# Two blocks of x laid in one run, four single blocks at the end of the first half of the GLU, and the second half's weights made among them

## The chip, the cores and the metric

The program runs on one core of one Trainium2 chip. Its time is the device time of the whole program in microseconds (us), from the first to the last instruction with what the device adds around them. Engines are written as in the profile: PE is TensorE (matrix products), with PEld its weight loads; DVE is VectorE, ACT is ScalarE, POOL is GpSimd, SP is SyncE, which only issues transfers. Each engine works through its own list of instructions in order, and waits where a semaphore tells it to.

## The reference, cut to what matters

```
x   = pooled_attention(q, k, v)              # 8 x 8 heads, 576 queries, 72 pooled keys -> x is 4608 x 512
h   = x @ w_in                               # 4608 x 2048
g   = (a0 + a1 h + a2 h^2 + a3 h^3) / (1 + |b0| |h| + |b1| h^2 + 1e-6)
x2  = g @ w_out                              # 4608 x 512
out = eight experts over x2                  # each token to one expert by a global ranking of the logits
```

The change lies in the second stage (h, g and x2, the "GLU" below), where it runs beside the end of the attention and up to the start of the routing.

## The kernel before, in words

**Blocks and halves.** The 4608 tokens are 18 blocks of 256 (NB, BLK). The 2048 columns of h are taken in two halves (`half` 0 and 1) of four pieces of 256 (`fp` 0 to 3). The first half is made while attention delivers x, and its partial result for a block goes to DRAM (`ya_d`); so does x itself (`store_x`, to `x_d`). The second half brings x and the partial result back (`load_b` on POOL's queue, `load_ya` on SP's), adds its own part and makes the router's logits.

**A step.** One step is one piece `fp` of one block ("single", both 128-column groups of the piece for 256 tokens) or one 128-column group of a piece for two blocks ("pair", 512 tokens). Both fill one accumulator tile of 128 x 512. A step has four parts: `mm_h` (PE: x times w_in, each factor split in a high and a low part, three products per 128 rows of x, names xh, xl, wih, wil); `act1` and `act2` (the rational function: five operations on ACT, five on DVE, two on POOL, which end in a high and a low tile of g, "hi" and "lo", written by DVE at L729 and by POOL at L345); and `mm_y` (PE: hi and lo times w_out, woh and wol, one group per 128 tokens, "tt": a single has two of them, a pair four). In `mm_y` L793 and L794 read hi, L791 reads lo.

**The ring of hi/lo tiles.** `act2` writes into the next tile of the list `mgl`: five tiles `mg`, and five more, `mgx`, from block 4 on; in the second half `mgx` is closed and five tiles `gd` are opened once block 2 begins (`swap_g`). A tile comes free when the last `mm_y` group that reads it is done.

**Single blocks and pairs.** In the first half blocks 0 to 3 run single and 4 to 17 as pairs; in the second half 0 and 1 single (SINGLE = 2), the rest as pairs. The four x tiles are `xt[0]` (xh0, xl0) and `xt[1]` (xh1, xl1), each of two blocks; block by block they lie behind one another, so a pair's `mm_h` reads two runs of 256 columns (`x()[:, :, c, :]`).

**The weights.** They come as 64-bit numbers in pieces (`load_w`), and `prep_w` turns a piece into a high and a low part: on ACT a conversion, on DVE three passes (L410, L412, L414), ACT again (the high part), POOL (the low part), and for w_out also transposes and small products on PE (L432, L436), which give the columns for the router. Each half has four pieces `fp` with four `prep_w` calls each (k = 0, 1 for w_in, 2, 3 for w_out). Of the second half's sixteen, eight are made in the first half's last blocks, into the pool `wpb`, which is opened when attention's pool `ap` has been closed (block 15 of the first half must be done with its `mm_h` first); fp = 2 and 3 go into the tiles of the first half's fp = 0 and 1 and wait for its last `mm_y`.

**What sets the order.** Operations are recorded with a cost, and a planner (`Order.run`) puts each engine's into one list by these costs, the priorities and the tiles' dependencies. So the code gives what depends on what, and the printed order of each engine what stands where.

Of the kernel before, what the change touches and what calls it, by code (L numbers as in the profile page):

```python
# [30 lines left out]
BLK = 256  # L31
# [15 lines left out]
V_POOL = 0  # L47
GBUFS, MGX, GDX = 5, 5, 5
PTB = 2
# [30 lines left out]
class Part:  # L80
# [5 lines left out]
    def __call__(self):  # L86
        return self.buf()[:, self.j]


# [201 lines left out]
class Kern:  # L291
# [163 lines left out]
    def init_att(self):  # L455
# [423 lines left out]
    def load_b(self, n):  # L879

        s, j = n // 2 % 2, n % 2
        extra = [("xr", m) for m in range(NB) if m % XBUFS == j] if n < 2 else []
        for k, x in enumerate(self.x1[s]):
            self.op("Pool", 1.05, lambda k=k, x=x: self.nc.gpsimd.dma_start(x()[:, j], self.x_d[n]()[:, k]), r=[("xd", n, k)],
                    w=[("xs", s, j, k)] + extra, nbytes=524288)

    def phase1(self):
        nc, op, b = self.nc, self.op, self.buf
        nc.scalar.preload_act_table_set("natural_log_exp_and_others")
        for p in ("wq", "stg", "pre"):  # L890
            self.open(p, side="right")
        for p in ("wp", "mp", "xp", "xq", "ap"):
            self.open(p)
# [22 lines left out]

        pieces = {h: [(h, fp, k) for fp in range(NFP) for k in range(4)] for h in range(2)}
        loads = {h: list(pieces[h]) for h in range(2)}

# [30 lines left out]
        for i, st in enumerate(steps):  # L950
            st["i"] = i
            n = st["blk"]
            if st["half"] == 0:
# [4 lines left out]
                if n == SPLIT and st["first"] and st["half"] == 0:  # L958
                    self.swap_m()
                while done < needed[st["blks"][-1]]:  # L960
                    assert slot()
                if done < len(att):
                    credit += 4 * RATE
                    while credit >= 1.0 and done < len(att):
                        credit -= 1.0
                        if not slot():
                            credit = 0.0
                            break
                elif not closed and NB - 3 in xdone:
                    closed = True  # L970
                    reads = [k for k in self.g.lastw if self.in_pool(k, ("ap", "xq"))]
                    reads += [("xr", m) for m in range(NB) if m % XBUFS > 1] + [("x", m, s, k) for m in self.xkeys for s in range(2) for k in self.xkeys[m]]
                    def swap():
                        self.close("ap")
                        self.close("xq")
                        self.open("wpb")
                        self.open("raw1")
                    assert not pieces[0]
                    op("Z", 0.0, swap, w=reads + ["swap"])
                    for fp in range(2):  # L980
                        self.w_tiles(1, fp, "wpb", f"b{fp}")
                        for t in self.w[1, fp]:
                            for k in range(4):
                                self.g.lastw[t, k] = self.g.lastw["swap"]
                    self.staging("raw1")
                    for t in (*self.raws, *self.wf, self.wm):
                        self.g.lastw[t] = self.g.lastw["swap"]
                    for _ in range(2):
                        self.load_w(*loads[1].pop(0))
                if closed and pieces[1] and pieces[1][0][1] < 2:  # L990
                    piece(1)
                st["x"] = self.xb[n % XBUFS] if len(st["blks"]) == 1 else self.xt[n // 2 % 2]
                st["xk"] = [k for m in st["blks"] for k in self.xk(m)]
            else:
                if st["first"] and n == 0:
# [16 lines left out]
                x = self.x1[n // 2 % 2]  # L1012
                st["x"] = x if len(st["blks"]) == 2 else tuple(Part(t, n % 2) for t in x)
                st["xk"] = [("xs", n // 2 % 2, m % 2, k) for m in st["blks"] for k in range(2)]
# [73 lines left out]
    def swap_m(self):  # L1088
# [5 lines left out]
        self.more_g("mx", "swapm", MGX, "mgx")  # L1094

    def free_x(self, s):

        key = ("freex", s)
        self.op("Z", 0.0, lambda: None, w=[("xs", s, j, k) for j in range(2) for k in range(2)] + [key])
        new = [tuple(View(x, lambda t, j=j, i=i: t[:, j].rearrange("p (i c) t -> p i (c t)", i=2)[:, i]) for i in range(2))  # L1100
               for x in self.x1[s] for j in range(2)]
# [4 lines left out]
    def swap_b(self):  # L1106

        def swap():
            self.close("mx")
# [4 lines left out]
        self.op("Z", 0.0, swap, w=[k for k in self.g.lastw if self.in_pool(k, ("wq", "stg", "mx"))] + ["swapb"])  # L1114
        self.mgl = [g for g in self.mgl if g[0].pool != "mx"]
        x = tuple(self.buf("yp", [128, 2, 4, BLK], F32R, x) for x in ("xhr", "xlr"))
        self.x1 = [self.xt[0], x]
        for j in range(2):
            for k in range(2):
                self.g.lastw["xs", 1, j, k] = self.g.lastw["swapb"]  # L1120
        self.yab = self.ring(2, "yp", [128, 2, 2 * GW], F32, "yab")
# [15 lines left out]
    def swap_g(self):  # L1137
# [4 lines left out]
        self.op("Z", 0.0, swap, w=[k for k in self.g.lastw if self.in_pool(k, ("raw1",))] + ["swapg"])  # L1142
        self.more_g("gd", "swapg", GDX, "gd")
        more = self.ring(MORE_R, "gd", [128, 2 * BLK], F32, "mrg")
        self.mr += more
# [592 lines left out]
TWO = 2  # L1738
PAIRS = SPLIT
Y0 = 4  # L1740
# [85 lines left out]
```

## Time and profile before

| | |
|---|---|
| time, median of 3 runs (lowest, highest) | 1531.73 us (1530.30, 1533.25) |
| profiled execution: time, span | 1529.58 us, 1527.8 us |
| mean granted TensorE clock | 0.982 |
| PE busy | 1454.1 us, 95% of the span |
| DVE busy | 1097.6 us, 72% |
| ACT, POOL busy | 883.3 us, 58%; 865.0 us, 57% |

A busy share is the part of the span in which the engine had at least one instruction under way. The granted clock is a share of TensorE's full speed; its two levels are 1.2 and 2.4 GHz, so that a mean between 0.5 and 1 says for how much of a stretch the lower one held.

### The profile page before, as it was taken

What the parts mean: (1) busy time and instruction counts of PE and PEld (TensorE: products, weight loads), DVE (VectorE), ACT (ScalarE), POOL (GpSimd) and SP (SyncE); (2) the same over time, 40 slices, a digit from 0 to 9 for tenths busy, and PEclk for the clock granted to TensorE, in tenths of its full rate; (3) what the DMA queues carried; (4) which work ended last, traced back from release to release, by engine and by line L of the source; (5) the groups of instructions that cost most, each with busy time, mean ns of one, the idle gap of its engine ahead of it and who ended that gap; (6) DMA issues with size and microseconds to landing.
All of it is one profiled execution on the core that took longest, in us unless ns stands there. A gap on an engine that the chain in (4) does not pass through costs nothing. (4 is left out here: it accounts for less than half of the span.)

```text
span 1527.8 us, 27162 instructions
## 1 busy us (share of the span) xinstructions
PE 1454.1 (95%) x9353; PEld 1307.1 (86%) x9353; DVE 1097.6 (72%) x3105; ACT 883.3 (58%) x2071; POOL 865.0 (57%) x806
## 2 busy tenths in 40 slices
PE   8899999999999999989999999995999999999996
PEld 6899978888898998978898998764888988988995
DVE  6897786858768678688777778888788778941220
ACT  5887886867868766656655456841343432443330
POOL 6776877557657456545544455652465554654421
PEclk9999999999999999989999999998999999999998
DMA  6663534132321324523231332003254333433300
GB/s 223 220 226 105 170 123 148 58 130 94 132 102 49 112 73 163 168 82 107 85 103 65 111 108 87 29 29 123 75 172 143 133 114 125 156 114 112 128 18 31
DMA packets 82023, 173.62 MB, mean 114 GB/s; under 512 B 10320, under 2 KB 37328, under 8 KB 81872
## 3 DMA queue, kind: packets, MB, share of 16 engines
q1 hardware_dynamic: 70800, 134.02, 25.9%
q0 software_dynamic: 11072, 37.76, 7.5%
q8 instruction: 74, 1.21, 0.3%
q14 instruction: 77, 0.63, 0.1%
HBM read 122.28 MB, written 49.46 MB: 112 GB/s over the span
## 5 line engine op out<-in xcount | busy, mean ns | idle before, releaser
L345 POOL TENSOR_TENSOR mq<-mq,ms 128x512 f32<-128x512 f32 x144 | 195.1, 1356 | 151.1 <-ACT mq L711 149.2
L693 PE MATMUL pa<-xh,wih 128*128 128x512 f32 (+1 forms) x448 | 166.7, 372 | 4.2 <-ACT wih L351 1.7
L693 PE MATMUL pa<-xh,wil 128*128 128x512 f32 (+1 forms) x448 | 159.3, 356 | 0.8 <-POOL wil L345 0.8
L693 PE MATMUL pa<-xl,wih 128*128 128x512 f32 (+1 forms) x448 | 158.9, 355 | 0.0
L708 ACT ACTIVATE ms<-pa 128x512 f32<-128x512 f32 x144 | 85.8, 596 | 120.1 <-PE pa L693 88.8
L1664 PE MATMUL pa<-yth,w1h 128*128 128x320 f32 (+1 forms) x512 | 145.2, 299 | 1.1 <-ACT yth L1635 0.7
L1664 PE MATMUL pa<-ytl,w1h 128*128 128x320 f32 (+1 forms) x512 | 144.3, 297 | 0.0
L1664 PE MATMUL pa<-yth,w1l 128*128 128x320 f32 (+1 forms) x512 | 143.9, 296 | 0.0
L713 DVE TENSOR_TENSOR mw<-mw,pa 128x512 f32<-128x512 f32 x144 | 97.9, 680 | 54.9 <-ACT mw L709 54.0
L793 PE MATMUL pa<-woh,mg 128*128 128x260 f32 (+1 forms) x484 | 131.1, 293 | 5.0 <-DVE mg L729 2.7
L794 PE MATMUL pa<-wol,mg 128*128 128x260 f32 (+1 forms) x484 | 129.0, 289 | 0.0
L1717 POOL DMA_INDIRECT out<-ob,ix x40 | 38.9, 972 | 152.5 <-ACT ob L1713 130.1
L345 POOL TENSOR_TENSOR mg<-mt,mr 128x512 fp32r<-128x512 f32 x68 | 89.0, 1310 | 63.8 <-DVE mt L733 36.1
L711 ACT ACTIVATE mq<-ms,scal 128x512 f32<-128x512 f32 x144 | 117.8, 818 | 10.0 <-DVE mt L731 9.9
L726 ACT ACTIVATE mr<-mq,scal 128x512 f32<-128x512 f32 x122 | 88.5, 725 | 50.4 <-POOL mq L345 39.5
L709 ACT ACTIVATE mw<-pa,scal 128x512 f32<-128x512 f32 x144 | 112.3, 780 | 1.6 <-PE pa L693 1.2
L1667 ACT ACTIVATE h2h<-pa 128x256 fp32r<-128x256 f32 (+1 forms) x128 | 51.4, 410 | 103.8 <-PE pa L1664 96.9
L565 ACT ACTIVATE ex<-pa,nm 128x72 f32<-128x72 f32 (+2 forms) x320 | 98.5, 325 | 20.0 <-DVE nm L556 13.8
L714 DVE SCALAR_TENSOR_TENSOR pa<-mw,scal,pa 128x512 f32<-128x512 f32 x144 | 107.7, 748 | 3.0 <-ACT ms L708 1.5
L733 DVE SCALAR_TENSOR_TENSOR mt<-pa,scal,mt 128x512 f32<-128x512 f32 x144 | 106.8, 742 | 0.9
L1698 PE MATMUL pa<-w2h,h2h 128*128 128x512 f32 x256 | 102.2, 399 | 0.0
L1290 DVE TENSOR_SCALAR_CACHE_REDUCE BJ<-BQ,cand 128x288 uint16<-128x288 f32 x217 | 99.5, 509 | 3.4 <-ACT BQ L1470 1.5
(325 smaller groups left out, 4865.1 us busy)
## 6 DMA issues: line engine op xcount, KB each, us to landing
wraw<-in_w SPq DMA_DIRECT2D x64, 512.0 KB, 3.6
ya_d<-ya SPq DMA_DIRECT2D x18, 520.0 KB, 3.3
yab<-ya_d SPq DMA_DIRECT2D x18, 520.0 KB, 4.3
kvraw<-in_kT SPq DMA_DIRECT2D x16, 576.0 KB, 4.2
x_d<-xh SPq DMA_DIRECT2D x18, 512.0 KB, 3.4
x_d<-xl SPq DMA_DIRECT2D x18, 512.0 KB, 4.6
y_d<-yb SPq DMA_DIRECT2D x18, 512.0 KB, 3.0
raw<-in_w_in SPq DMA_DIRECT2D x16, 512.0 KB, 4.8
```

The costliest lines, as they stand in the source:

```text
L345: self.g.either({"Pool": (p_tt(n), lambda: nc.gpsimd.tensor_tensor(out(), x(), y(), op=alu)), "DVE": (c_tt(n), lambda: nc.vector.tensor_te ...
L565: op("Act", c_act(NK, 0, 1, 1), lambda h=h: nc.scalar.activation(e()[:n, h, :], sv()[:, h, :], AF.Exp, bias=nm()[:n, h:h + 1], accum_out=s ...
L693: nc.tensor.matmul(o, w()[:, c, f], x()[:, :, c, :] if two else x()[:, c, :], start=c == 0 and k == 0, stop=c == 3 and k == 2)
L709: op("Act", c_act(N, 0, 2), lambda: nc.scalar.activation(w(), ph(), AF.Identity, scale=self.a3(), bias=self.a2()), r=hk + self.sk, w=[w])
L711: op("Act", c_act(N, 1, 2), lambda: nc.scalar.activation(q(), s(), AF.Identity, scale=self.b1a(), bias=self.b0a()), r=[s] + self.sk, w=[q])
L714: op("DVE", c_stt(N), lambda: nc.vector.scalar_tensor_tensor(ph(), w(), self.a1(), ph(), op0=ALU.add, op1=ALU.mult), r=[w], w=hk)
L733: op("DVE", c_stt(N), lambda: nc.vector.scalar_tensor_tensor(t(), w(), self.a0(), t(), op0=ALU.add, op1=ALU.subtract), r=[(w, 0), self.hri ...
L793: nc.tensor.matmul(o, hi()[:, f], w(woh), start=first, stop=False)
L794: nc.tensor.matmul(o, hi()[:, f], w(wol), start=False, stop=False)
L1290: D(.43, lambda: self.nc.vector.tensor_scalar(j(), key(), cand(), None, op0=ALU.is_ge, op1=ALU.add, accum_out=self.cnt()[:, col:col + 1]), ...
L1664: nc.tensor.matmul(ps()[:, 0:n], w()[:, c, fs], x()[:, c, :], start=i == 0, stop=i == 11)
L1698: nc.tensor.matmul(ps(), x()[:, t], w()[:, f % 2, :], start=f == 0 and i == 0, stop=False)
```

## The change

Five things change together. (1) An x tile now holds the two blocks side by side for each 128 rows (`[128, 4, 2, BLK]` for `[128, 2, 4, BLK]`), so a pair's `mm_h` reads one run of 512 columns; writing a block, storing it and loading it touch four runs of 256 for one of 1024. (2) Blocks 14 to 17 of the first half run single (PEND = NB - 4), and the five `mgx` tiles are given back at block 14 (`swap_x`), so the ring has five tiles from there until block 2 of the second half. (3) `ap` is closed at block 14, once attention has been recorded to its end, and the second half's weights start there: ten pieces go into blocks 14 to 17 by one a step, some more in block 17's last steps, and the rest is recorded at the start of the second half. fp = 2 takes the tiles of w_in's fp = 0 and two new tiles in `wpb`, fp = 3 those of w_in's fp = 1 and of w_out's fp = 0; for fp = 2 w_out's pieces come first. (4) The second half's x goes to `xt[1]` first and then `xt[0]`, instead of `xt[0]` and two tiles xhr, xlr of its own. (5) Three tiles `gd` instead of five, and w_out's tiles of the first half's fp = 1 serve as two more.

```diff
-GBUFS, MGX, GDX = 5, 5, 5
+GBUFS, MGX, GDX = 5, 5, 3
...
+class Col(Part):
+
+
+    def __call__(self):
+        return self.buf()[:, :, self.j]
...
-        self.xt = [tuple(b(p, [128, 2, 4, BLK], F32R, f"{x}{k}") for x in ("xh", "xl")) for k, p in enumerate(("xp", "xq"))]
-        self.xb = [tuple(Part(x, k % 2) for x in self.xt[k // 2]) for k in range(XBUFS)]
+        self.xt = [tuple(b(p, [128, 4, 2, BLK], F32R, f"{x}{k}") for x in ("xh", "xl")) for k, p in enumerate(("xp", "xp"))]
+        self.xb = [tuple(Col(x, k % 2) for x in self.xt[k // 2]) for k in range(XBUFS)]
...
-            o = ph().rearrange("p (b t) -> p b t", b=2) if two else ph()[:, BLK * j:BLK * j + BLK]
+            o = ph() if two else ph()[:, BLK * j:BLK * j + BLK]
...
-                    nc.tensor.matmul(o, w()[:, c, f], x()[:, :, c, :] if two else x()[:, c, :],
+                    nc.tensor.matmul(o, w()[:, c, f], x()[:, c].rearrange("p b t -> p (b t)") if two else x()[:, c, :],
...
-        parts = alone + [(0, [n], range(NFP)) for n in range(SPLIT, PAIRS)] + [(0, [n, n + 1], range(NFP)) for n in range(PAIRS, NB, 2)]
+        parts = alone + [(0, [n], range(NFP)) for n in range(SPLIT, PAIRS)] + [(0, [n, n + 1], range(NFP)) for n in range(PAIRS, PEND, 2)]
+        parts += [(0, [n], range(NFP)) for n in range(PEND, NB)]
...
+                if n == PEND and st["first"]:
+                    while rest:
+                        rest.pop(0)()
+                    self.swap_x()
...
-                elif not closed and NB - 3 in xdone:
+                elif not closed and n >= PEND:
...
+                    free = [self.buf("wpb", [128, 2, 2, GW], F32R, f"{x}b2") for x in ("woh", "wol")]
+                    self.w[1, 2] = [*self.w[0, 0][:2], *free]
+                    self.w[1, 3] = [*self.w[0, 1][:2], *self.w[0, 0][2:]]
...
-                if closed and pieces[1] and pieces[1][0][1] < 2:
+                if closed and (len(pieces[1]) > 6 or len(pieces[1]) > 4 and n == NB - 1 and st["fp"] > 0 or len(pieces[1]) > 2 and n == NB - 1 and st["fp"] > 1):
                     piece(1)
...
-                    for fp in (2, 3):
-                        self.w[1, fp] = self.w[0, fp - 2]
-                while pieces[1] and pieces[1][0][1] <= st["fp"]:
-                    piece(1)
+                    while pieces[1]:
+                        piece(1)
...
+    def swap_x(self):
+        self.op("Z", 0.0, lambda: self.close("mx"), w=[k for k in self.g.lastw if self.in_pool(k, ("mx",))] + ["swapx"])
+        self.mgl = [g for g in self.mgl if g[0].pool != "mx"]
...
-        x = tuple(self.buf("yp", [128, 2, 4, BLK], F32R, x) for x in ("xhr", "xlr"))
-        self.x1 = [self.xt[0], x]
...
+        self.x1 = self.xt[::-1]
...
+        w = self.w[0, 1][2:]
+        self.op("Z", 0.0, lambda: None, w=[(t, k) for t in w for k in range(4)] + ["freew"])
+        new = [tuple(View(t, lambda t, i=i: t.rearrange("p c g d -> p (c g d)")[:, 512 * i:512 * i + 512]) for i in range(2)) for t in w]
...
-PAIRS = SPLIT
+PAIRS, PEND = SPLIT, NB - 4
```

ACT, DVE, POOL and SP have as many operations as before. PE's matmuls go from 9343 to 9535. Each engine's order is the same up to the first `mm_h` of block 14 in the first half (about 503 us in the trace) and again from block 2's last piece of the second half (about 715 us); between them it is another one. In the rows below lines of after.py stand seven higher (L693 is L700, L791 to L794 are L798 to L801, L345 is L352, L884 is L891).

On PE, where block 14 begins in the first half, the list before has a pair's `mm_h` (xh1, xl1 hold blocks 14 and 15) among the last `mm_y` groups of the pair 12 and 13.

```order
L552 MATMUL pa7_274<-kbd0_100,qraw0_102 128x144 x2
L693 MATMUL pa5_233<-xh1_795,wih0_145 128x512
L693 MATMUL pa5_233<-xl1_809,wih0_145 128x512
L693 MATMUL pa5_233<-xh1_795,wil0_191 128x512
L791 MATMUL pa4_231<-woh3_1595,mg4_1460 128x260
```

With the change the same place has the first products of block 14 alone, half as wide and twice as many.

```order
L559 MATMUL pa7_271<-kbd0_97,qraw0_99 128x144 x2
L700 MATMUL pa5_230<-xh1_792,wih0_142 128x256
L700 MATMUL pa5_230<-xl1_806,wih0_142 128x256
L700 MATMUL pa5_230<-xh1_792,wil0_188 128x256
L700 MATMUL pa5_230<-xh1_792,wih0_142 128x256
L700 MATMUL pa5_230<-xl1_806,wih0_142 128x256
L700 MATMUL pa5_230<-xh1_792,wil0_188 128x256
L798 MATMUL pa4_228<-woh3_1592,mg4_1457 128x260
```

The weights' names now say which piece they are: a pair's row carries 512 tokens against the weights loaded for it, a single's row 256. Over the whole program 192 rows of 128x512 have become 384 of 128x256.

On PE, where the second half begins (wihb0 is its first weight, woh3 the first half's last), the list before has the first `mm_h` of block 0 right behind products that read the last piece's hi and lo of the pair 16 and 17.

```order
L791 MATMUL pa5_233<-woh3_1595,mgx4_2868 128x260
L791 MATMUL pa3_197<-woh3_1595,mgx4_2868 128x260
L793 MATMUL pa5_233<-woh3_1595,mg1_981 128x260
L794 MATMUL pa5_233<-wol3_1607,mg1_981 128x260
L793 MATMUL pa3_197<-woh3_1595,mg1_981 128x260
L794 MATMUL pa3_197<-wol3_1607,mg1_981 128x260
L693 MATMUL pa4_231<-xh0_353,wihb0_6152 128x256
```

With the change that `mm_h` stands directly behind the last `mm_h` of the first half, and the `mm_y` groups of block 17 from its piece 1 on follow it.

```order
L700 MATMUL pa4_228<-xh0_350,wil3_1490 128x256
L439 MATMUL pa1_145<-ident_112,wf1_6171 128x128 x4
L700 MATMUL pa2_191<-xh1_792,wihb0_6150 128x256
L700 MATMUL pa2_191<-xl1_806,wihb0_6150 128x256
L700 MATMUL pa2_191<-xh1_792,wilb0_6166 128x256
L700 MATMUL pa2_191<-xh1_792,wihb0_6150 128x256
L700 MATMUL pa2_191<-xl1_806,wihb0_6150 128x256
L700 MATMUL pa2_191<-xh1_792,wilb0_6166 128x256
L800 MATMUL pa3_194<-woh1_625,mg4_1457 128x260
```

The first step of the second half now stands ahead of the `mm_y` of block 17's pieces 1 to 3 instead of among the pair's last ones, and its x comes from xh1 and xl1.

On POOL, where x of the second half's first two blocks is loaded (x_d0, x_d1), the list before has the loads among the low parts of the weights and of `mgx` tiles, late in the pair 16 and 17.

```order
L884 DMA xh0_353<-x_d0_594 128x1024
L345 TENSOR_TENSOR wolb1_6607<-wf0_6139,wohb1_6594 128x2x256
L345 TENSOR_TENSOR mgx3_2796<-mt0_889,mr1_934 128x512
L884 DMA xh0_353<-x_d1_813 128x1024
L884 DMA xl0_362<-x_d0_594 128x1024
L345 TENSOR_TENSOR mgx4_2868<-mt1_992,mr0_835 128x512
L884 DMA xl0_362<-x_d1_813 128x1024
```

With the change they go to xh1 and xl1, in pieces of four runs, among the low parts of block 14's and 15's steps, whose tiles are now the five `mg` alone.

```order
L891 DMA xh1_792<-x_d0_591 128x4x256
L352 TENSOR_TENSOR mg2_1158<-mt0_886,mr1_931 128x512
L352 TENSOR_TENSOR mq2_1002<-mq2_1002,ms1_872 128x512
L891 DMA xl1_806<-x_d0_591 128x4x256
L352 TENSOR_TENSOR mg3_1343<-mt1_989,mr0_832 128x512
L352 TENSOR_TENSOR mq0_763<-mq0_763,ms0_735 128x512
L352 TENSOR_TENSOR mg4_1457<-mt2_1192,mr1_931 128x512
L352 TENSOR_TENSOR mq1_891<-mq1_891,ms1_872 128x512
L352 TENSOR_TENSOR wilb0_6166<-wf0_6130,wihb0_6150 128x512
```

The first load stands some thirty rows earlier in POOL's list (row 409 for 442), ahead of the first low part of a second-half weight instead of behind the sixth.

## Rows read from the trace of the kernel before

**Rows 1.** The page: engines' busy time and share; granted clock in 40 slices, tenths.

```profile
PE 1454.1 (95%) x9353; PEld 1307.1 (86%) x9353; DVE 1097.6 (72%) x3105; ACT 883.3 (58%) x2071; POOL 865.0 (57%) x806
...
PEclk9999999999999999989999999998999999999998
```

**Rows 2.** Stretches, us: busy time (instructions) of each engine, granted clock, DMA.

```profile
core 0: us, PE busy (x) PEld busy (x) DVE busy (x) ACT busy (x) POOL busy (x), PEclk, DMA share, GB/s
...
505.00:692.00 187.00, 175.38 (x1188) 161.90 (x1187) 142.11 (x259) 118.82 (x223) 100.60 (x88) 0.96 0.37 124
...
580.00:596.00 16.00, 12.25 (x83) 11.22 (x82) 16.00 (x26) 12.64 (x23) 14.27 (x13) 0.95 0.42 138
596.00:604.00 8.00, 7.99 (x59) 7.50 (x59) 5.44 (x11) 3.68 (x10) 4.33 (x5) 0.88 0.76 252
604.00:620.00 16.00, 16.00 (x136) 16.00 (x136) 6.33 (x12) 7.38 (x15) 6.37 (x7) 1.00 0.59 199
...
636.00:662.00 26.00, 19.87 (x110) 17.29 (x109) 18.06 (x29) 18.29 (x34) 14.84 (x14) 0.82 0.38 122
662.00:692.00 30.00, 28.27 (x196) 26.06 (x196) 26.43 (x67) 10.41 (x16) 11.14 (x8) 0.99 0.21 71
...
960.00:1000.00 40.00, 40.00 (x177) 30.81 (x176) 39.42 (x81) 37.17 (x60) 27.88 (x20) 1.00 0.08 26
```

**Rows 3.** Waits of PE from 560 to 690 us: total, times, longest.

```profile
PE pa L432 <- DVE wf L414: 2.6, 1, 2.6
PE pa L693 <- ACT wih L351: 1.7, 1, 1.7
```

**Rows 4.** Timeline of PE at the half switch: start, duration, group, idle before.

```profile
588.69 0.39 PE L793 MATMUL pa<-woh,mgx 128*128 128x260 f32 x1 [0.85 <-DVE mgx L729]
...
594.32 0.71 PE L791 MATMUL pa<-woh,mgx 128*128 128x260 f32 x2 [1.59 <-POOL mgx L345]
...
599.72 0.28 PE L693 MATMUL pa<-xh,wihb 128*128 128x256 f32 x1
...
600.31 0.28 PE L693 MATMUL pa<-xh,wilb 128*128 128x256 f32 x1
```

**Rows 5.** Timeline of PE in a pair's products of 512.

```profile
568.49 0.39 PE L693 MATMUL pa<-xh,wil 128*128 128x512 f32 x1
...
572.22 0.40 PE L693 MATMUL pa<-xh,wih 128*128 128x512 f32 x1
```

**Rows 6.** Timeline of PE in the experts' products of 512, from one run.

```profile
1400.30 0.39 PE L1698 MATMUL pa<-w2h,h2h 128*128 128x512 f32 x1
...
1403.29 0.39 PE L1698 MATMUL pa<-w2h,h2l 128*128 128x512 f32 x1
1403.51 1.98 PE L1695 MATMUL pa<-w2l,h2h 128*128 128x512 f32 x8
```

**Rows 7.** Groups of PE over the span, shapes apart: count, busy, mean ns.

```profile
L693 PE MATMUL pa<-xh,wih 128*128 128x512 f32 x288 | 118.1, 410 | 1.9 <-ACT ex L565 1.2 <-DVE pth L594 0.5
...
L693 PE MATMUL pa<-xhr,wihb 128*128 128x512 f32 x64 | 25.8, 403 | 0.2 <-DVE mt L733 0.2
```

**Rows 8.** Groups of the weight loads over the span.

```profile
L693 PEld LDWEIGHTS pa<-xh,wih 128*128 128x128 f32 x448 | 85.4, 191 | 15.5 <-ACT ex L565 2.0 <-ACT wih L351 1.9 <-ACT mr L728 0.9
```

**Rows 9.** Groups of DVE and POOL, 540 to 720 us, shapes apart.

```profile
L714 DVE SCALAR_TENSOR_TENSOR pa<-mw,scal,pa 128x512 f32<-128x512 f32 x26 | 19.4, 747 | 0.2
L713 DVE TENSOR_TENSOR mw<-mw,pa 128x512 f32<-128x512 f32 x26 | 17.6, 678 | 21.1 <-ACT mw L709 21.1
L410 DVE TENSOR_SCALAR pa<-wm 128x512 int32<-128x512 int32 x16 | 11.0, 689 | 5.0 <-ACT wm L409 4.8
...
L345 POOL TENSOR_TENSOR mgx<-mt,mr 128x512 fp32r<-128x512 f32 x5 | 6.5, 1291 | 3.5 <-DVE mt L733 3.0 <-ACT mr L728 0.5
```

**Rows 10.** Transfers of x: count, ns to issue min/median/max, first and last start.

```profile
L355 SPq DMA_DIRECT2D x_d<-xh x18: 320/359/559, 42.6 to 524.4; - x18
...
L884 POOL DMA_DIRECT2D xh<-x_d x10: 537/580/757, 591.0 to 932.8; - x10
...
DMA to landing us min/median/max: 2.6/4.5/8.8
```

More of the change, by code (lines that the diff above doesn't have):

```diff
@@ L881, in load_b @@
         s, j = n // 2 % 2, n % 2
-        extra = [("xr", m) for m in range(NB) if m % XBUFS == j] if n < 2 else []
+        extra = [("xr", m) for m in range(NB) if m % XBUFS == 2 - 2 * s + j] if n < 4 else []
         for k, x in enumerate(self.x1[s]):
-            self.op("Pool", 1.05, lambda k=k, x=x: self.nc.gpsimd.dma_start(x()[:, j], self.x_d[n]()[:, k]), r=[("xd", n, k)],
+            self.op("Pool", 1.05, lambda k=k, x=x: self.nc.gpsimd.dma_start(x()[:, :, j], self.x_d[n]()[:, k]), r=[("xd", n, k)],
                     w=[("xs", s, j, k)] + extra, nbytes=524288)
@@ L891, in phase1 @@
             self.open(p, side="right")
-        for p in ("wp", "mp", "xp", "xq", "ap"):
+        for p in ("wp", "mp", "xp", "ap"):
             self.open(p)
@@ L917, in phase1 @@
         pieces = {h: [(h, fp, k) for fp in range(NFP) for k in range(4)] for h in range(2)}
+        pieces[1][8:12] = [(1, 2, k) for k in (2, 3, 0, 1)]
         loads = {h: list(pieces[h]) for h in range(2)}
@@ L968, in phase1 @@
                             break
-                elif not closed and NB - 3 in xdone:
+                elif not closed and n >= PEND:
                     closed = True
-                    reads = [k for k in self.g.lastw if self.in_pool(k, ("ap", "xq"))]
-                    reads += [("xr", m) for m in range(NB) if m % XBUFS > 1] + [("x", m, s, k) for m in self.xkeys for s in range(2) for k in self.xkeys[m]]
+                    reads = [k for k in self.g.lastw if self.in_pool(k, ("ap",))]
+                    reads += ["swapx"]
                     def swap():
                         self.close("ap")
-                        self.close("xq")
                         self.open("wpb")
@@ L984, in phase1 @@
                                 self.g.lastw[t, k] = self.g.lastw["swap"]
+                    free = [self.buf("wpb", [128, 2, 2, GW], F32R, f"{x}b2") for x in ("woh", "wol")]
+                    self.w[1, 2] = [*self.w[0, 0][:2], *free]
+                    self.w[1, 3] = [*self.w[0, 1][:2], *self.w[0, 0][2:]]
+                    for t in free:
+                        for k in range(4):
+                            self.g.lastw[t, k] = self.g.lastw["swap"]
                     self.staging("raw1")
@@ L1012, in phase1 @@
                 x = self.x1[n // 2 % 2]
-                st["x"] = x if len(st["blks"]) == 2 else tuple(Part(t, n % 2) for t in x)
+                st["x"] = x if len(st["blks"]) == 2 else tuple(Col(t, n % 2) for t in x)
                 st["xk"] = [("xs", n // 2 % 2, m % 2, k) for m in st["blks"] for k in range(2)]
@@ L1099, in free_x @@
         self.op("Z", 0.0, lambda: None, w=[("xs", s, j, k) for j in range(2) for k in range(2)] + [key])
-        new = [tuple(View(x, lambda t, j=j, i=i: t[:, j].rearrange("p (i c) t -> p i (c t)", i=2)[:, i]) for i in range(2))
+        new = [tuple(View(x, lambda t, j=j, i=i: t[:, 2 * j + i].rearrange("p b t -> p (b t)")) for i in range(2))
                for x in self.x1[s] for j in range(2)]
@@ L1108, in swap @@
         def swap():
-            self.close("mx")
             self.close("stg")
@@ L1113, in swap @@
             self.open("yp", side="right")
-        self.op("Z", 0.0, swap, w=[k for k in self.g.lastw if self.in_pool(k, ("wq", "stg", "mx"))] + ["swapb"])
-        self.mgl = [g for g in self.mgl if g[0].pool != "mx"]
-        x = tuple(self.buf("yp", [128, 2, 4, BLK], F32R, x) for x in ("xhr", "xlr"))
-        self.x1 = [self.xt[0], x]
-        for j in range(2):
-            for k in range(2):
-                self.g.lastw["xs", 1, j, k] = self.g.lastw["swapb"]
+        self.op("Z", 0.0, swap, w=[k for k in self.g.lastw if self.in_pool(k, ("wq", "stg"))] + ["swapb"])
+        self.x1 = self.xt[::-1]
         self.yab = self.ring(2, "yp", [128, 2, 2 * GW], F32, "yab")
@@ L1143, in swap_g @@
         self.more_g("gd", "swapg", GDX, "gd")
+        w = self.w[0, 1][2:]
+        self.op("Z", 0.0, lambda: None, w=[(t, k) for t in w for k in range(4)] + ["freew"])
+        new = [tuple(View(t, lambda t, i=i: t.rearrange("p c g d -> p (c g d)")[:, 512 * i:512 * i + 512]) for i in range(2)) for t in w]
+        for t in (x for g in new for x in g):
+            self.g.lastw[t] = self.g.lastw["freew"]
+        self.mgl = new + self.mgl
         more = self.ring(MORE_R, "gd", [128, 2 * BLK], F32, "mrg")
```

## The prediction

> **What bounds the kernel now.** I read the page first: PE is busy for 95% of the span and the other engines for 57 to 72%, and the granted clock is full in all but three of the 40 slices [rows 1]. So the time is PE's list of products at its pitch, plus the few places where PE stands still or runs at the lower clock. Then I cut the trace into stretches. The reader is to see that the change's own stretch, 505 to 692 us, is one of those places: PE works 175.38 of its 187 us, so 11.62 are idle, nearly all of them in 580–596 (3.75), 636–662 (6.13) and 662–692 (1.73) [rows 2]. In the same stretches the granted clock is 0.95, 0.88, 0.82 and 0.99 (580–596, 596–604, 636–662, 662–692), which is time at 1.2 GHz after PE had been waiting; as work lost while busy that is 12.25 × 0.05 + 7.99 × 0.12 + 19.87 × 0.18 + 28.27 × 0.01 = 5.5 us. Together some 17.1 us are lost at the passage from the first half to the second.
>
> What PE waits for there is told by the chain of waits and the timeline: passes of DVE over a weight piece (2.6 us in one), the high part of a weight on ACT (1.7), DVE's hi (0.85) and POOL's lo (1.59) of a step [rows 3, 4]. So it is short of ready operands, not of work: DVE is busy 16.00 of 16 us in 580–596, and then 6.33 of 16 in 604–620 [rows 2]. It has its weight pieces and its steps in two heaps with a hole between, the hole being the last `mm_y` of the pair 16 and 17, in which PE works 16.00 of 16 us and DVE has no new accumulator to read. Elsewhere a full DVE costs nothing: in 960–1000 it is busy 39.42 of 40 us and PE 40.00 [rows 2].
>
> **The change part by part.** The sum is made against the profiled execution, 1529.58 us, that is 2.15 below the median of the runs; the forecast is put on the median, 1531.73.
>
> *One run of 512 for a pair.* A pair's products start 0.233 us apart: 568.49 to 572.22 holds sixteen steps, 3.73/16 [rows 5]. The experts' products of the same 128x512 from one run start 0.230 apart where operands alternate (1400.30 to 1403.29, thirteen steps) and (1.98 − 0.39)/7 = 0.227 apart in a group of eight [rows 6]. The 128x512 products of `mm_h` are 3 × (288 + 3 × 64) = 1440 (three other groups of 64 for each of the three products are like the one shown) [rows 7]; 192 of them become 384 halves, so 1248 remain. The bounds are 0 (the pitch is not set by the runs) and 1248 × 0.006 = 7.5 us. I take 2.5 ns, near the alternating rows, which mm_h resembles most: **−3.1 us**.
>
> A rule speaks against this term. The Trainium skill, "Advanced Engine Details and Errata", section "SBUF Cachelines", says that access runs at full rate as long as following accesses hit the same 16-byte line. Two runs of 1 KB lose nothing by that, the term would be 0 and the sum 3.1 us less; the rows show a difference of 3 to 6 ns, but between different lines of code, so they do not refute it.
>
> *Halves for wholes.* 384 products of 256 at 0.119 (599.72 to 600.31 holds five steps, 0.59/5 [rows 4]) are 45.7 us, 192 of 512 at 0.2315 (a little under the 0.233 above) are 44.4: **+1.3 us**. Every one of the 192 more products brings a weight load of 0.191 us [rows 8]; at a pitch of 0.119 such loads plainly lie over other loads and products, so they cost nothing more.
>
> The Trainium skill, "TensorE: Matmul & The Clock Gate", section "The mechanism", has loads overlap products in flight only when their row groups differ, which full 128-row weights never do. By it the 192 loads would be paid. It is a rival below, at a small chance, since a pitch of 0.119 beside a load of 0.191 contradicts it.
>
> *The passage between the halves.* Here the waits of 17.1 us are spread out. I counted each engine's operations in the two printed orders between block 14 and block 2, in pieces of 70 to 140 of PE's operations, with durations from the rows: a step is five passes of DVE of 0.68 to 0.75 (3.7 us), a weight piece three of 0.69 [rows 9], and PE's by the pitches above. Before, PE against DVE, in us: 29.4/27.9, 20.4/13.3, 28.0/37.1, 14.2/7.6, 33.7/39.1, 38.3/41.9. DVE has 9.1 + 5.4 + 3.6 = 18.1 more than PE in three of them, which is near the 17.1 that the trace loses. After: 19.9/8.7, 33.3/32.7, 29.6/29.9, 24.7/20.2, 24.8/27.5, 30.4/33.6, 27.4/28.9, an excess of 0.3 + 2.7 + 3.2 + 1.5 = 7.7. In proportion 17.1 × 7.7/18.1 = 7.3 us stay if the clock falls again, and 11.62 × 7.7/18.1 = 4.9 if it does not. I take 6 left: **−11.1 us**. The bounds are nothing lost (−17.1) and as much as now (0).
>
> *What costs nothing, and its cover.* Loads of x for block 0 and 1 are issued some thirty rows of POOL's list earlier and take 0.58 us each to issue, stores 0.34 to 0.36, landing within 2.6 to 8.8 us [rows 10]; in four runs of 1 KB instead of one of 4 they may take longer. Behind a load on POOL stand the low parts of the steps (1.29 us each [rows 9]), and PE waits for those; the cover is POOL's idle time, 187 − 100.60 us in this stretch [rows 2]. If it were gone, eight loads of 0.58, 4.6 us, would be on the path. A load now waits until block 14's or 15's last product has read xh1; that lies a whole block before the second half's first product. Pool `ap` is closed earlier, behind attention's last operation, and the first weights can only start earlier with it. The ring of ten after `swap_g` stays ten. From block 14 to block 1 it has five tiles: a single step's product finds its hi and lo if the tile's last reader is done some 0.75 + 0.74 × 2 + 1.29 = 3.5 us and the hand-overs earlier. PE has a step's `mm_h` (24 × 0.119 = 2.9 us) and its `mm_y` (about 3) to do meanwhile, so it is thin but covered.
>
> Sum: −3.1 + 1.3 − 11.1 = −12.9, so 1516.7 for an execution like the profiled one and **1519 us** on the median.
>
> **The rivals.** *The passage closes and the run gives its full price.* For it: DVE's work in 505–692 is 142.11 us and would fill 84% of 170, and 960–1000 shows that PE can run through at 99% [rows 2]. Against: the excess of 7.7 above. −7.5 + 1.3 − 17.1 = −23.3, some **1508 us**.
>
> *The waits only move.* Eight pieces of weights now stand between the end of block 16 and block 1, in the stretches of 24.8/27.5 and 30.4/33.6 above; if each hole there brings PE to the lower clock again, the passage loses what it lost. Also if the change doesn't do what it says (the order's gain is in the planner's costs, not on the chip), this is the case. −3.1 + 1.3 = −1.8: **1530 us**, the same.
>
> *The ring of five starves PE: slower.* From block 14 to block 1 six single blocks make 24 steps, and `act2` of a step waits until `mm_y` has freed the oldest tile, while the next `mm_y` waits for that `act2`. If each such round costs what the two waits of that kind cost now, (0.85 + 1.59)/2 = 1.2 us [rows 4], it is 24 × 1.2 = 29 us against the 12.9 gained: +16, **1548 us**. It decides for slower from (12.9 + 3.1)/24 = 0.67 us a step on. Against: the tile that a step needs was last read a whole step before, by the sum of 3.5 us above.
>
> *The loads of weights are paid.* 192 × 0.191 = 36.7 us, so −12.9 + 36.7 = +24: **1556 us**. Against: the pitch of 0.119.
>
> **How the numbers follow.** My forecast (1512 to 1526) has a chance of 0.66, the closed passage 0.14, moved waits 0.12, the ring of five 0.07, the paid loads 0.01. A difference under 0.2%, 3.1 us, can't be told from none. Faster is 0.66 + 0.14 and 0.01 of the moved waits that still end below 1528.7: 0.81; the same 0.11; slower 0.08. The range reaches from most of the closed passage to most of the moved waits, 1508 to 1530; the 1548 and 1556 are left out.
>
> **What would show it.** Right: a pair's products 0.230 apart or less, PE over 96% busy between 505 us and the start of the routing's keys, the granted clock at 1.00 in most of it, DVE near 84% without a hole of 6 in 16 us. The residual would be waits for weight passes in block 17 and block 0. Wrong: waits of L798 or L800 on DVE and POOL at every step of blocks 14 to 17 (the ring), a pitch of 256-wide products above 0.119 (the loads), or a pair's products still 0.233 apart (the run). The prediction fails upward if the clock drops in more than one place after 580 us, and downward if routing's start, where before PE also waits, is moved by an earlier second half.

## The result, and the profile after

The changed kernel takes 1508.53 us (median of 4 runs, 1504.52 to 1510.97) against 1532.40 us of the kernel before beside it (4 runs), a ratio of 0.9844 with a 95% interval of 0.9818 to 0.9869: 23.9 us faster. The forecast was 1519 in a range of 1508 to 1530, so the time came in at the range's lower edge, 10 us from the forecast. The profiled execution took 1510.97 us, its span is 1509.2.

First the page: engines' busy time and share, and the granted clock in 40 slices, to be read against [rows 1].

```profile
span 1509.2 us, 27443 instructions
PE 1450.5 (96%) x9545; PEld 1313.8 (87%) x9545; DVE 1099.2 (73%) x3105; ACT 881.9 (58%) x2071; POOL 872.9 (58%) x806
...
PEclk9999999999999999999999999997999999999999
```

PE's busy time hardly fell (1454.1 to 1450.5), though it has 192 products more: of the 18.6 us by which the span is shorter, 15.0 are idle time of PE (73.7 to 58.7). The lower clock that stood in the slices at the passage between the halves is gone; the one low slice left is the routing's start.

The passage in stretches of busy time, columns as in [rows 2]:

```profile
520.00:580.00 60.00, 59.91 (x504) 59.70 (x503) 54.66 (x84) 44.84 (x83) 41.70 (x36) 1.00 0.53 151
580.00:640.00 60.00, 59.14 (x499) 58.92 (x498) 48.70 (x80) 46.55 (x93) 37.73 (x32) 1.00 0.47 139
640.00:700.00 60.00, 58.47 (x371) 52.45 (x371) 53.56 (x109) 37.04 (x58) 35.91 (x30) 1.00 0.33 89
```

PE is idle for 2.48 of 180 us where it was for 11.62 of 187, the granted clock is 1.00 throughout, and DVE is busy 87% of it (156.92). Before, it was busy for 40% of 604–620 [rows 2]; now its emptiest 16 us of this stretch are at 57%:

```profile
580.00:596.00 16.00, 16.00 (x138) 16.00 (x137) 9.19 (x18) 10.79 (x24) 6.56 (x6) 1.00 0.29 100
```

The list of PE's waits from 500 to 700 us (total, times, longest) has three entries left, the first of them routing's:

```profile
PE pa L1296 <- DVE ext L1294: 1.1, 1, 1.1
PE pa L800 <- DVE wf L421: 0.9, 1, 0.9
PE pa L800 <- DVE mt L740: 0.4, 1, 0.4
```

How long the passage takes is read between two transfers that stand at the same place of both programs: the 13th and the 23rd of those that write or read the partial result `ya_d` (start, us). In the kernel before, on SP:

```profile
497.52 0.32 SPq L355 DMA_DIRECT2D ya_d<-ya  x1
...
722.24 0.42 SPq L355 DMA_DIRECT2D yab<-ya_d  x1
```

In the changed kernel:

```profile
496.48 0.33 SPq L362 DMA_DIRECT2D ya_d<-ya  x1
...
705.13 0.41 SPq L362 DMA_DIRECT2D yab<-ya_d  x1
```

So 224.7 us became 208.7, 16.0 less. What PE lost between the two transfers accounts for it; before, then after:

```profile
497.52:722.24 224.72, 213.10 (x1427) 196.10 (x1426) 173.58 (x311) 147.26 (x274) 122.03 (x107) 0.97 0.34 115
```

```profile
496.48:705.13 208.65, 206.17 (x1602) 199.32 (x1601) 173.85 (x311) 145.87 (x274) 124.15 (x107) 1.00 0.42 124
```

Before, PE was idle for 11.6 us and, by the trace's clock records, busy for 12.5 us at the lower of its two clock levels, which costs half of that time, 6.3 us: together 17.9 us lost. After, it is idle for 2.5 us and never at the lower level. DVE's work is the same to 0.3 us, in a stretch that is 16 us shorter.

The second place is the very end, which no part of the forecast spoke of. The last scatter of results on POOL, before and then after:

```profile
1516.52 0.90 POOL L1717 DMA_INDIRECT out<-ob,ix  x1 [3.42 <-DVE ob L1716]
```

```profile
1505.29 0.90 POOL L1737 DMA_INDIRECT out<-ob,ix  x1 [3.42 <-DVE ob L1736]
```

The span ends at 1527.8 and 1509.2, so 11.3 us after that instruction's start before and 3.9 us after the change: 7.4 less. Nearly all of that time lies in one instruction of POOL, a drain at the program's end, which the page doesn't count as busy: by the trace's records it starts 0.2 us ahead of that scatter, in both, and lasts 10.69 us before and 3.34 after. No transfer runs in most of that time, as the DMA view of the kernel before shows from 1516 to 1528 us in 40 slices (tenths busy, GB/s):

```profile
DMA  0000006920000000000000000000000000000000
GB/s 0 0 0 0 0 0 150 218 68 0 0 0 0 0 0 0 0 0 0 0 0 0 0 0 0 0 0 0 0 0 0 0 0 0 0 0 0 0 0 0
```

The scatter's data are through before 1519; POOL ends eight us later. 16.0 + 7.4 = 23.4 us.

That this is so near to the 23.9 us between the medians is in part chance. The two profiled executions themselves differ by 18.6 us only (the one before lay 2.8 us under its median, the one after 2.4 above), because two further stretches stand beside the 23.4: 1.0 us less up to the 13th transfer, and 5.9 us more from the 23rd to the last scatter. In the second trace of each kernel (e1, e4) the same stretches give −17.8 and −7.4, with 2.1 more at the start and 1.9 more at the later one. From the 23rd transfer to the last scatter it is 794.3 to 795.5 us in the four traces of the order before and 795.3 to 800.2 in nine of the changed one; what costs this was not looked into.

### The profile page after: what moved, and what is told of

The parts are those of the page before. It is cut to its first block, busy times and chain, and to the rows that moved or that the text cites. A ratio compares the mean times of both kernels' runs of the same rounds, so it can differ in the third digit from the quotient of the medians.

```text
span 1509.2 us, 27443 instructions
## 1 busy us (share of the span) xinstructions
PE 1450.5 (96%) x9545; PEld 1313.8 (87%) x9545; DVE 1099.2 (73%) x3105; ACT 881.9 (58%) x2071; POOL 872.9 (58%) x806
## 3 DMA queue, kind: packets, MB, share of 16 engines
q0 software_dynamic: 24896, 37.76, 9.0%
## 5 line engine op out<-in xcount | busy, mean ns | idle before, releaser
L352 POOL TENSOR_TENSOR mq<-mq,ms 128x512 f32<-128x512 f32 x144 | 195.4, 1358 | 146.2 <-ACT mq L718 144.3
L700 PE MATMUL pa<-xh,wih 128*128 128x256 f32 (+1 forms) x576 | 202.1, 351 | 2.6 <-ACT ex L572 1.2
L700 PE MATMUL pa<-xh,wil 128*128 128x256 f32 (+1 forms) x576 | 194.8, 338 | 0.0
L700 PE MATMUL pa<-xl,wih 128*128 128x256 f32 (+1 forms) x576 | 194.5, 338 | 0.0
L352 POOL TENSOR_TENSOR mg<-mt,mr 128x512 fp32r<-128x512 f32 x78 | 101.0, 1295 | 70.0 <-DVE mt L740 34.2
L801 PE MATMUL pa<-wol,mg 128*128 128x260 f32 (+1 forms) x492 | 127.5, 285 | 0.0
L700 PEld LDWEIGHTS pa<-xh,wih 128*128 128x128 f32 x576 | 109.0, 189 | 14.1 <-ACT ex L572 2.0
L700 PEld LDWEIGHTS pa<-xh,wil 128*128 128x128 f32 x576 | 108.6, 189 | 12.7
L700 PEld LDWEIGHTS pa<-xl,wih 128*128 128x128 f32 x576 | 109.1, 189 | 9.1
```

The costliest lines, as they stand in the source:

```text
L352: self.g.either({"Pool": (p_tt(n), lambda: nc.gpsimd.tensor_tensor(out(), x(), y(), op=alu)), "DVE": (c_tt(n), lambda: nc.vector.tensor_te ...
L700: nc.tensor.matmul(o, w()[:, c, f], x()[:, c].rearrange("p b t -> p (b t)") if two else x()[:, c, :], start=c == 0 and k == 0, stop=c == 3 ...
L801: nc.tensor.matmul(o, hi()[:, f], w(wol), start=False, stop=False)
```

## The experiments

The rival theories after the result were: where the 16 us at the passage come from (weights made early, single blocks, or both), whether the ring of five costs anything, what one run of 512 is worth, and whether the end's 7.4 us belong to the change or to chance. "Passage" below is the time between the two transfers shown above, "end" the time from the start of the last scatter to the end of the span, each from the profiled execution. In two traces of one kernel the passage is 224.7 and 226.5 us (before, e1) and 208.7 twice (the change, e4), so that differences under 2 us in that column say nothing. What PE loses in the passage, counted as above, is 17.9 and 20.1 us in the two traces of the kernel before and 2.5 in both of the change; in e5, e6, e7, e9 and e11 it is 12.3, 17.8, 3.9, 13.2 and 22.2. The rest of the passage is 206.0 to 207.1 us in all nine, so the passage is as long as the loss makes it. Each ratio is to runs of the kernel before taken beside that run; their medians lie between 1531.39 and 1532.44 us, so that times of different rows compare to about 1 us.

| kernel | time, us | ratio to before (95%) | passage | end |
|---|---|---|---|---|
| before | 1532.40 | | 224.7 | 11.3 |
| the change | 1508.53 | 0.9844 (0.9818 to 0.9869) | 208.7 | 3.9 |
| e1 before again | 1530.70 | 0.9990 (0.9976 to 1.0003) | 226.5 | 11.3 |
| e2 new layout of x alone | 1525.22 | 0.9958 (0.9940 to 0.9976) | 226.6 | 3.9 |
| e3 change, old layout of x | 1515.99 | 0.9906 (0.9874 to 0.9937) | 207.9 | 11.3 |
| e4 change again | 1509.17 | 0.9842 (0.9807 to 0.9876) | 208.7 | 3.9 |
| e5 change, pairs 14 to 17 | 1513.83 | 0.9883 (0.9863 to 0.9903) | 218.2 | 3.9 |
| e6 change, weights late | 1526.39 | 0.9969 (0.9958 to 0.9980) | 224.8 | 3.9 |
| e7 change, ring of four | 1510.62 | 0.9855 (0.9837 to 0.9873) | 210.8 | 3.9 |
| e8 before, loads halved | 1528.44 | 0.9970 (0.9951 to 0.9988) | 227.9 | 5.2 |
| e9 change, eight pieces early | 1519.07 | 0.9905 (0.9885 to 0.9925) | 219.6 | 3.9 |
| e10 change, loads in eight pieces | 1529.34 | 0.9986 (0.9971 to 1.0001) | 216.2 | 6.7 |
| e11 change, single 16 and 17 only | 1531.03 | 0.9983 (0.9970 to 0.9996) | 229.3 | 3.9 |
| e12 change, single 12 to 17 | 1506.58 | 0.9835 (0.9809 to 0.9862) | (other start) | 3.9 |

**e1, the kernel before once more.** No edit.

> The kernel before, unchanged. If the 10.7 us that POOL's last drain took in the trace of before belong to the program, they are there again (10 to 11 us) and the time is 1530 to 1533; if they are a matter of the single execution, the drain is anywhere from 3 to 11 us and the time moves with it.

1530.70 us, and the drain again 10.69 us. **e4, the changed kernel once more**, likewise without an edit:

> The changed kernel again, beside the two above on the same chip: 1505 to 1511, drain of POOL at the end 3 to 4 us if it belongs to the program, anything from 3 to 11 us if it doesn't.

1509.17 us, the drain 3.34 us again. The two kernels that were traced twice show it at the same length both times, to 0.01 us: it belongs to the program.

**e2, the new layout of x alone, and e3, the change without it.**

```diff
-        self.xb = [tuple(Part(x, k % 2) for x in self.xt[k // 2]) for k in range(XBUFS)]
+        self.xb = [tuple(Col(x, k % 2) for x in self.xt[k // 2]) for k in range(XBUFS)]
...
-            self.op("Pool", 1.05, lambda k=k, x=x: self.nc.gpsimd.dma_start(x()[:, j], self.x_d[n]()[:, k]), r=[("xd", n, k)],
+            self.op("Pool", 1.05, lambda k=k, x=x: self.nc.gpsimd.dma_start(x()[:, :, j], self.x_d[n]()[:, k]), r=[("xd", n, k)],
```

These two of the change's lines with the tiles' shape and the reads in `mm_h` in e2; the same in reverse in e3.

> The kernel before with the new layout of x alone (one run of 512 for a pair, loads and stores of a block in four pieces of 1 KB). The prediction's term: pair products 0.230 apart, 3 us faster (1529). The rival that the runs don't matter: 0.2315 apart, 0 us from it. If the loads in four pieces are also what shortens POOL's last drain from 10.7 to 3.3 us, 7 us faster (1525) with the pitch unchanged.

> The changed kernel with x's old layout (two runs of 256 for a pair, loads in one piece of 4 KB). The prediction's term: 3 us slower than the change (1511 to 1512). Runs don't matter: as the change (1508 to 1509). Loads in four pieces shorten the drain: 7 us slower (1516), drain 10.7 us.

e2 is 6.7 us faster than the kernel before beside it (1531.94), e3 6.8 us slower than the change beside it (e4, 1509.17). Both are the third expectation: the drain is 3.34 us with the new layout and 10.69 with the old one, whatever else the kernel has. The pitch did not move. A pair's products in e2:

```profile
404.23 0.39 PE L700 MATMUL pa<-xh,wih 128*128 128x512 f32 x1
...
406.10 0.39 PE L700 MATMUL pa<-xh,wil 128*128 128x512 f32 x1
```

That is eight steps in 1.87 us, 0.234 apart, and 0.233 in [rows 5]; over all pair products the mean start-to-start time below 0.3 us is 0.2316 in e2 and 0.2316 before. The rival that the runs don't matter holds for the products. What the layout gave is the shorter drain; that the loads on POOL's queue move it, without the layout, is shown by e8 below.

**e5, pairs instead of single blocks.**

```diff
-        parts += [(0, [n], range(NFP)) for n in range(PEND, NB)]
+        parts += [(0, [n, n + 1], range(NFP)) for n in range(PEND, NB, 2)]
```

> The changed kernel with blocks 14 to 17 of the first half as two pairs; ring of five, early weights and everything else as changed. If the recovered waits (about 16 us at the passage) come from the weights made early, it stays at 1508 to 1511 (192 products of 512 for 384 of 256 give 1 us back, the hole of the last pair's products costs a few). If the single blocks are what fills the hole and makes a ring of five enough, 8 to 20 us slower than the change (1517 to 1529), with waits for hi and lo tiles and the lower clock back.

5 us slower, passage 9.5 longer, between the two expectations. By the code two further things differ from the change. A pair's eight steps need eight tiles until its end; with five, the products for tt 1 to 3 read tiles that later steps have already written, so this kernel makes that part of the computation from other data, and the waits for the right tiles are not in this time. And the rule that puts further pieces, after the tenth, into block 17's last steps asks for a step that begins with block 17, which a pair never does: here they fall to the start of the second half. So e5 does not tell what pairs alone would cost here.

**e6, single blocks with the weights late.**

```diff
-                if closed and (len(pieces[1]) > 6 or len(pieces[1]) > 4 and n == NB - 1 and st["fp"] > 0 or len(pieces[1]) > 2 and n == NB - 1 and st["fp"] > 1):
+                if closed and n >= NB - 2 and len(pieces[1]) > 8:
```

> The changed kernel, single blocks as changed, but only eight weight pieces in blocks 16 and 17 of the first half and eight at the start of the second, as before. If the early weights are what removes the waits: 8 to 16 us slower (1517 to 1525), with waits of TensorE for weight passes and the lower clock. If the single blocks alone do it: as the change, 1508 to 1511.

17.9 us slower than the change, a little past the first expectation, and the passage is that of before (224.8 for 224.7), with what PE loses in it:

```profile
496.25:721.09 224.84, 212.34 (x1603) 203.99 (x1602) 174.58 (x311) 147.27 (x274) 124.53 (x107) 0.97 0.39 115
```

Single blocks by themselves gave nothing. Its waits of PE from 500 to 720 us (total, times, longest), the four longest:

```profile
PE pa L700 <- DVE mt L740: 4.1, 2, 3.4
PE pa L700 <- POOL wil L352: 2.4, 2, 1.5
PE pa L800 <- DVE mg L736: 2.3, 1, 2.3
PE pa L798 <- POOL mg L352: 1.6, 1, 1.6
```

and the stretch in which they lie, with the clock:

```profile
620.00:640.00 20.00, 14.52 (x103) 13.46 (x101) 16.12 (x25) 11.85 (x21) 9.53 (x8) 0.91 0.40 131
640.00:660.00 20.00, 13.66 (x73) 11.79 (x72) 15.05 (x23) 14.14 (x27) 15.32 (x14) 0.77 0.44 106
```

These are the waits for steps and weight passes of [rows 3, 4], at other lines, with the clock of [rows 2] down again.

**e9, eight pieces early and eight at the second half's start.**

```diff
-                if closed and (len(pieces[1]) > 6 or len(pieces[1]) > 4 and n == NB - 1 and st["fp"] > 0 or len(pieces[1]) > 2 and n == NB - 1 and st["fp"] > 1):
+                if closed and len(pieces[1]) > 8:
```

> The changed kernel with eight weight pieces made as early as changed (one a step from block 14 on), and the other eight only at the start of the second half. If it is the early start of the first eight that removes the waits, 1509 to 1511. If it is that the start of the second half has few pieces left, the heap of eight pieces (24 DVE passes, 16.5 us) before TensorE's single blocks 0 and 1 costs 4 to 10 us: 1513 to 1519.

10.5 us slower than the change, passage 10.9 longer, 5.2 shorter than e6's. So of the 16 us about 5 come from starting the first eight at block 14 and about 11 from making more than eight before the second half (by the medians of the times 7.3 and 10.5). PE's longest waits from 480 to 720 us are for a step in the heap and for a weight pass:

```profile
PE pa L800 <- DVE mg L736: 4.8, 1, 4.8
PE pa L439 <- DVE wf L421: 2.8, 2, 2.4
```

DVE is busy 14.61 and 12.00 of 20 us in the two stretches where PE loses most:

```profile
620.00:640.00 20.00, 15.03 (x112) 14.62 (x112) 14.61 (x26) 12.03 (x24) 8.46 (x8) 0.84 0.58 204
640.00:660.00 20.00, 17.61 (x103) 15.75 (x102) 12.00 (x25) 14.10 (x27) 14.58 (x13) 0.81 0.45 106
```

so there too it is not DVE's sum of work. The chain within the heap is not taken apart here: from 490 to 720 us DVE also waits 3.4 us for ACT's conversions of weight pieces, and ACT 1.6 us for their transfers. The clock after the waits falls again (0.84, 0.81).

**e11 and e12, fewer and more single blocks.**

```diff
-PAIRS, PEND = SPLIT, NB - 4
+PAIRS, PEND = SPLIT, NB - 2
```

(NB - 6 in e12.)

> The changed kernel with only blocks 16 and 17 single at the end of the first half (14 and 15 a pair with a ring of ten), so the weights' memory is free two blocks later and seven or eight pieces fall to the start of the second half. If pieces must start at block 14 for the waits to go: 10 to 16 us slower than the change (1519 to 1525). If the single blocks at the very end are enough: 1508 to 1512.

> The changed kernel with blocks 12 to 17 single. 96 more products of 512 become 192 of 256, 0.6 us more by pitch; the waits left (about 2.5 us) may go if weights start earlier, though attention's memory must be free first. 1507 to 1511 by what was measured so far; 2 to 6 us slower if blocks 12 and 13, where attention still runs, are short of tiles with a ring of five.

e11 is 22.5 us slower than the change, beyond either expectation, with a passage of 229.3: the eight steps of blocks 16 and 17 hold at most eight of the sixteen pieces, and the rest stands in one heap, as in e6. Its longest wait of PE from 480 to 720 us is for a weight's high part:

```profile
PE pa L700 <- ACT wih L358: 3.8, 1, 3.8
```

e12 is at 1506.58, with an interval that covers the change's: starting yet earlier gives 2 us by the medians, which the spread of the runs doesn't tell from nothing, and 2.48 idle us were all that was left. It beats the kernel before, but not clearly the change.

**e7, a ring of four.**

```diff
         self.mgl = [g for g in self.mgl if g[0].pool != "mx"]
+        self.spare = self.mgl.pop(0)
```

(It comes back in `swap_g`.)

> The changed kernel with four hi/lo tiles instead of five from block 14 of the first half until block 2 of the second. If five are thin but covered, as the prediction had it, four are not: 24 steps at 0.5 to 1.2 us, 12 to 29 us slower (1521 to 1538). If a step's tile was free long before, nothing: 1508 to 1511.

1510.62 us, passage 2.1 longer. Even four tiles cost at most a tenth of a microsecond a step (2.1/24), so five are not thin at all.

**e8 and e10, other sizes of the loads on POOL's queue.**

```diff
-            self.op("Pool", 1.05, lambda k=k, x=x: self.nc.gpsimd.dma_start(x()[:, j], self.x_d[n]()[:, k]), r=[("xd", n, k)],
+            self.op("Pool", 1.05, lambda k=k, x=x: [self.nc.gpsimd.dma_start(x()[:, j, c:c + 2], self.x_d[n]()[:, k, c:c + 2]) for c in (0, 2)], r=[("xd", n, k)],
```

(In e10 the changed kernel's load is split by tokens, 0 to 127 and 128 to 255.)

> The kernel before with each load of x on POOL's queue issued as two transfers of 2 KB a partition (15680 packets on that queue for 11072; the new layout has 24896). If POOL's last drain gets shorter with the number of packets on its queue, it lies between 3.3 and 10.7 us, or at 3.3, and the time is up to 7 us under 1531; if only the strided pieces of the new layout do it, it stays at 10.7 and the time at 1531 to 1533.

> The changed kernel with each load of x on POOL's queue issued as two transfers, so in eight pieces of 512 bytes a partition instead of four of 1 KB. If more packets on that queue shorten POOL's last drain (10.7, 4.6 and 3.3 us at 11072, 16256 and 24896 packets), it is 3.3 or a little less, and the time 1508 to 1512 with POOL busier by 36 issues of 0.6. If the drain follows something that comes round with the number of packets, it is anywhere up to 10.7 and the time up to 1516.

In e8 the drain is 4.64 us, though the layout of x is the old one: it follows what is queued on POOL, not the strided tile. The time fell by only 3.0 us against the kernel before beside it, where the end is 6.0 us shorter. In its trace the 13th transfer stands at 500.3 us (before 497.5, e1 497.7) and the passage is 227.9; but the 13th transfer lies anywhere from 494.1 to 501.5 us in the traces that have it at the same place, so whether the halved loads cost the other 3 us is not shown. In e10 it is 6.12 us, so it does not simply fall with the packets: by the pages' queue q0, 10.69 us at 11072 packets, 4.64 at 16256, 3.34 at 24896 and 6.12 at 43904. Its time, 1529.34 us, missed both expectations: 20.8 us slower than the change. The 36 further issues on POOL cost 7.5 us at the passage and 10.7 us from the 23rd transfer to the start of the routing's keys. There PE is idle for 6.2 us more than with the change, by waits of this kind (700 to 1010 us); the other 4.5 stand in the trace as a longer busy time:

```profile
PE pa L798 <- POOL mg L352: 3.5, 6, 0.9
PE pa L798 <- POOL gd L352: 1.3, 3, 0.9
```

while POOL is busy in little over half of the time:

```profile
720.00:980.00 260.00, 253.76 (x1539) 223.46 (x1538) 194.02 (x421) 149.37 (x234) 151.54 (x131) 1.00 0.36 86
```

## Why the prediction was right or wrong

**The passage: right mechanism, sized too small.** The step was "−11.1 us" with 6 us left. Between the two transfers 17.9 us were lost before, a little more than the 17.1 of the forecast, whose window (505 to 692 us) was shorter and whose clock terms add to 5.4 and not 5.5; 2.5 us are lost after, and 16.0 went. So the mis-sized term is the 6 us left: 2.5. It came from the excess of DVE over PE by stretches, 7.7 us in the proportion 7.7/18.1, and this was not a forecast of waits. A likely reason is that DVE's steps run ahead through the ring, so that an excess of 3 us in one stretch is covered by work done in the one before; no run here tests that. The signs that the forecast named for it came: the granted clock is 1.00, DVE is busy for 83% of the passage (173.85 of 208.65), and a wait for a weight pass is among the few that are left. That the weights' place is the cause is shown by e6 (late: the whole passage back) and e9 (eight early: two thirds of it back); e11, with a heap of that kind and two blocks fewer single, agrees. That the single blocks as such gave nothing is e6 too. By the code they are what allows a ring of five, and so the room for the weights; a pair has as many steps for its two blocks.

**One run of 512: wrong.** "−3.1 us" measured 0. The step that failed is the comparison of one line's pitch with another's (0.233 against 0.230 and 0.227): the difference does not belong to the runs, since e2 changed these and the pitch stayed at 0.2316; what makes it was not looked into. The rule in the Trainium skill, "Advanced Engine Details and Errata", section "SBUF Cachelines", that following accesses to the same line run at full rate, is what the trace of e2 agrees with (0.2316 us with one run and with two); the forecast set it aside.

**Halves for wholes: right.** The products of 256 still start 0.119 us apart (median) beside weight loads of 0.189 us each, and with all 192 of the additional ones e6's passage is as long as before; the rival of paid loads (+36.7 us) is out. In the changed kernel, 37 steps in 4.40 us, and the loads over the span:

```profile
559.80 0.28 PE L700 MATMUL pa<-xl,wih 128*128 128x256 f32 x1
...
564.20 0.29 PE L700 MATMUL pa<-xh,wil 128*128 128x256 f32 x1
```

```profile
L700 PEld LDWEIGHTS pa<-xh,wih 128*128 128x128 f32 x576 | 109.0, 189 | 14.1 <-ACT ex L572 2.0 <-ACT mr L735 0.9 <-ACT mr L733 0.8
```

The forecast's own row gives 0.118 (0.59/5), which would make the term +0.9 and not +1.3; both are too small to be seen. The rule of the Trainium skill, "TensorE: Matmul & The Clock Gate", section "The mechanism", that loads overlap only where row groups differ, does not describe this stream. The same section also lets a load into the background weight buffer go ahead of products in flight, which the forecast left out; with that the trace agrees (0.119 beside 0.189).

**The ring of five: right that it is covered.** e7 shows it with one tile less. The rival of a starved ring would have needed 0.67 us a step; four tiles cost at most 0.09.

**What cost nothing: wrong on two counts.** The loads in four pieces were looked at for their issue and landing alone. Their issue became longer (0.79 us for 0.58 of [rows 10], the median of the changed kernel's 36) and cost nothing that can be seen, as forecast; but they shortened the program's last drain by 7.35 us, the largest miss of the sum, which stands behind no row that the forecast read. And "POOL's idle time" as the cover was too coarse: in e10 POOL is 58% busy and PE waits for it all the same, for low parts (L352) that stand behind the issues in POOL's list.

So, from the forecast of 1519 to the measured 1508.5: the run gave 0 for −3.1 (+3.1), the passage with the additional products −16.0 for −9.8 (−6.2), the end −7.35 for nothing (−7.35), together −10.5. The passage and the end are from the profiled executions, whose other stretches differ too, as said in the section on the result, so that the sum closes better than it is known. The range held by 0.5 us, because the rival of the closed passage (1508 us) was in it. That this rival's time was right to 1 us is luck: its 7.5 us for the run of 512 came from the drain instead.

## What to carry to other kernels

Where PE waits at a change of phase, count how many steps lie between the point at which the next phase's preparation may begin and the point at which it is due, and put one piece into each step; with too few steps for the pieces (e11) or the rest in one heap (e9), most of the loss stays. Before a price is taken from another line's pitch, make the one change by itself: a difference of 1% between lines was no property of the operand's layout. Read the last instructions of the trace as well as its bulk: from the last transfer to the end of the span it may be several microseconds that a change of some unrelated transfer moves.

## What the hardware showed that was not expected

The drain of POOL at the end of the program lasts 10.69, 4.64, 3.34 or 6.12 us according to what was loaded over POOL's queue earlier in the program, the last of these loads some 580 us before, and to 0.02 us the same wherever the loads were the same (10.69 three times with the old ones, 3.33 to 3.35 nine times with the new). That it depends on the loads is shown by e2, e3, e8 and e10; in which way it does, by the number of descriptors, by where in a queue the last one lies or by something else, is open: four points are not enough, and no run varied the count alone in small steps.
